# Decay attention, then two feed-forward stages, on one core: scores of the first eight head pairs by fp32 products, transposes on two row halves, reciprocals turned by VectorE

## The chip, the core and the metric

The kernel runs on one core of a Trainium2 chip. Its time is device microseconds (us) of one execution, and the number to move is the median over runs: 971.85 us before the change (three runs, 971.4 to 974.48). TensorE (PE) multiplies matrices into eight PSUM banks; VectorE (DVE), ScalarE (ACT) and GpSimd (POOL) work on tiles in SBUF and PSUM; SyncE (SP) issues the DMA transfers. Each engine runs its own list of instructions in order, and semaphores tie the lists together.

## The reference

Attention over 4 batches of 8 heads, 576 positions of 64 numbers each, with a decay that comes from gates f; then two feed-forward stages over 2304 rows.

```python
scores = np.matmul(q, k.transpose(0, 1, 3, 2)) / np.sqrt(D)      # D = 64, S = 576
cum = np.cumsum(np.log(np.clip(f, 0.0001, 1.0)), axis=-1)
scores = np.where(causal, -1e9, scores + cum[:, :, :, None] - cum[:, :, None, :])
attn = np.exp(scores - np.max(scores, axis=-1, keepdims=True))
x = np.matmul(attn / (np.sum(attn, axis=-1, keepdims=True) + 1e-09), v)   # -> 2304 x 512
...
x = act1(x @ w_in) @ w_out            # 512 -> 2048 -> 512
x = act2(x @ w_in2) @ w_out2          # 512 -> 2048 -> 512
```

## The kernel before

Two heads of one batch make a pair, and there are 16 pairs. The 576 queries of a head are five blocks: four of 128 and a last one of 64. The last blocks of both heads are stacked into one tile (`both` in the code), so a pair has nine tiles of 128 query rows. For each tile there are these steps, named as in the code:

- **S**, scores into PSUM (L460 for the stacked tile, L469 for the others). q and k were split beforehand into a high and a low fp32r part (`hi` on ACT, L415; `lo` on DVE or POOL, L419), and a score is three products, low x high, high x low and high x high. For the stacked tile q goes in with zeros beside each head (`diag`, L422), on all 128 rows of the array. For the other tiles the two heads have 64 contracted rows each, and two matmuls run on the two row halves of the array, into two banks. A tile takes only the keys up to its diagonal: 512, 384, 256 or 128.
- **M**, the row maximum (L509, DVE), which also adds the decay and the mask from the tile `cb`. Pair 0 has no `cb`: there the decay is a fourth product with the tile `ct`, which four small DMAs fill.
- **E**, the exponential with its row sum (L521, ACT).
- **T**, the transpose of the probabilities (L533, PE): per 128 keys one 128x128 fp32 matmul against the identity, into one bank; two such banks are in turn (`TB_` = 2). **C** copies the bank to SBUF, on ACT or DVE (L381, L383).
- **V**, probabilities by values (L570, PE), plain fp32, the two heads side by side on two column halves of the array; **O** copies the result out.
- **R**: reciprocals of the row sums (L594, L595), transposed on PE (L599), copied by ACT (L604), stored by one DMA (L607), loaded back broadcast over partitions (L614, L615) and multiplied in by POOL (L619).

Beside the attention PE has filler work: for the first two column chunks the first layer of stage one with four of its sixteen weight blocks (h, L758) and their share of the second layer (a, L839), 96 + 96 matmuls of 512 columns. Weights come as 64-bit numbers and are turned into fp32 by ACT and DVE (L93 to L113), much of it beside the attention. Then the two feed-forward stages follow (L758, L852, L854).

The order of the instructions on each engine is not the order of the code. Each step is a task with a key, a duration, what it depends on and which buffers it takes; a planner (`plan`) puts the tasks out by expected time and key, and `NUDGE`, a list of (first task, count, shift), moves keys. The emitted order is fixed; on the chip an engine waits where its next instruction is not ready.

At the start f is loaded, clipped (L655), turned into logarithms (L706) and summed up (L658); PE meanwhile runs 26 matmuls on zeros (L652).

Of the kernel before, what the change touches and what calls it, by code (L numbers as in the profile page):

```python
# [18 lines left out]
def kernel(ctx, tc, qT, kT, v, f, w_in1, w_out1, w_in2, w_out2, a, b, out):  # L19
# [21 lines left out]
    W_EARLY = 4  # L41
    W_MID = 5
# [4 lines left out]
    SB, TB_, OB, RB = 4, 2, 2, 2  # L47
    KM, KEX, KT, KC, KV, KR, KX, PKL, LK, FE, FS = 0.0, 1.0, 4.0, 4.0, 7.0, 2.0, 9.0, 7.0, 14.0, 170.0, 40.0
    I_K, I_Q = 4.4, 5.2
    CS = 12.0  # L50
    WARM, WARM2 = 12, 14
# [7 lines left out]
    ACT.preload_act_table_set("natural_log_exp_and_others")  # L59

    ident = const.tile([P, P], F32, name="ident")
    POOL.memset(ident[:], 1.0)
    POOL.affine_select(
        out=ident[:], in_=ident[:], compare_op=ALU.is_equal, fill=0.0, base=0,
        pattern=[[-1, P]], channel_multiplier=1,
    )
# [75 lines left out]
    def w_load(m, g, half):  # L142
# [19 lines left out]
    tri = ap1.tile([P, 512], F32, name="tri")  # L162
    tri2 = ap1.tile([P, 256], F32, name="tri2")
    POOL.memset(tri[:], 0.0)
    POOL.memset(tri2[:], 0.0)
    POOL.affine_select(
        out=tri[:, 384:512], in_=tri[:, 384:512], compare_op=ALU.is_ge, fill=-BIG, base=0,
        pattern=[[-1, P]], channel_multiplier=1,
    )
    for j in range(2):  # L170
        t = tri2[j * QB:(j + 1) * QB, 192:256]
        POOL.affine_select(
            out=t, in_=t, compare_op=ALU.is_ge, fill=-BIG, base=0, pattern=[[-1, QB]], channel_multiplier=1,
        )

    kt, qt = [[[ap1.tile([P, S], F32R, name=f"{x}{y}{n}") for y in "hl"] for n in range(2)] for x in "kq"]
    qd = [[ap1.tile([P, P], F32R, name=f"qd{y}{n}") for y in "hl"] for n in range(2)]


    cb = [ap1.tile([P, 3, S], F32, name=f"cb{n}") for n in range(2)]
    ct = [ap1.tile([P, S], F32R, name="ct0")]
# [3 lines left out]
    rt_ = [ap1.tile([P, P], F32, name=f"rt{n}") for n in range(2)]  # L190
    for n in range(2):
        POOL.memset(vt[n][0:QB, NC - 1, :], 0.0)
        POOL.memset(rt_[n][:], 0.0)
    one, oned = [ap1.tile([P, P], F32R, name=f"one{x}") for x in range(2)]
    half = ap1.tile([P, 2], F32, name="half")
    POOL.memset(half[:], 0.0)
    POOL.memset(oned[:].bitcast(F32), 0.0)
    for j in range(2):
        pp = slice(j * QB, (j + 1) * QB)
        POOL.memset(half[pp, j:j + 1], 1.0)  # L200
        POOL.memset(oned[j * QB:j * QB + 2, pp].bitcast(F32), 1.0)
    POOL.memset(one[:].bitcast(F32), 1.0)
    POOL.memset(ct[0][:].bitcast(F32), 0.0)
# [8 lines left out]
    def load_pair(pr, x):  # L212
        if x < 2:
            t = ap2.tile([P, S], F32, tag=("ks", "qs")[x], name=f"{'kq'[x]}s{pr}")
            SP.dma_start(t[:], (kT, qT)[x][pr])
        else:
            t = vt[pr % 2]
            SP.dma_start(
                t[:, 0:NC - 1, :], v[pr, 0:(NC - 1) * P, :].rearrange("(c p) d -> p c d", p=P)
            )  # L220
            SP.dma_start(t[QB:P, NC - 1, :], v[pr, (NC - 1) * P:S, :])
        nat[pr, x] = t

# [48 lines left out]
    MOVE, LAND = 1.4, 1.4  # L272
# [116 lines left out]
    xa = {}  # L389

    def tasks_of_pair(pr):
# [3 lines left out]
        c_ = ct[0]  # L395
# [25 lines left out]
        def diag(y, eng):  # L421
            ENGINES[eng].tensor_tensor(  # L422
                out=(qdh, qdl)[y][:].rearrange("p (x s) -> p x s", x=2),
                in0=(qh, ql_)[y][:, S - QB:S].bitcast(F32).unsqueeze(1).to_broadcast([P, 2, QB]),
# [6 lines left out]
        else:  # L431
            T("ldc", -99, "sp", [(0.55, 0.05)] * 4, lambda: load_c(pr), ((0, "c"),), ("cb",))
# [6 lines left out]
        T("qd0", kk + 3, ways, [0.24, 0.4], [lambda e=e: diag(0, e) for e in ways], ("qhi",))  # L439
        T("qd1", kk + 3, ways, [0.24, 0.4], [lambda e=e: diag(1, e) for e in ways], ("qlo",))  # L440
# [728 lines left out]
```

## Time and profile before

| | |
|---|---|
| median of three runs | 971.85 us (971.4 to 974.48) |
| span of the profiled execution | 969.2 us; the median is 2.65 us above it |
| PE busy | 956.1 us, 99% of the span |
| DVE, ACT, POOL busy | 707.6 us, 629.7 us, 436.0 us |
| last V ends, last filler follows | 215.15 us, to 220.94 us |
| from there to the end | PE busy 744.28 us of 745 us |

An engine's busy time counts an instruction from its start to its end, and matmuls overlap, so a busy PE may still be waiting between starts. How much a run of matmuls costs is read from start to start, or from the chain of work that ended last, in which each piece lasts until the next one starts.

### The profile page before, as it was taken

The page shows a single profiled execution, that of the slowest core. Times are in us where ns is not written, and L with a number is a line of the kernel's source. Part 1 is how long each engine was busy: PE and PEld are TensorE (multiplying, and loading weights), DVE is VectorE, ACT ScalarE, POOL GpSimd, SP SyncE. Part 2 cuts the span into 40 slices and gives each one's busy share as a digit, 9 for nine tenths or more (in the row PEclk, how much of TensorE's full clock was granted, in tenths as well). Part 3 has the DMA queues.
Part 4 walks back from the last instruction along what each step waited for, and adds up shares of the span by engine and source line. Part 5 has one row for each costly group of instructions (what it writes and reads, how often), then busy time and mean ns, then how long its engine had stood idle before and what let it go on. Part 6 is the DMA issues. An engine that isn't in the chain of part 4 may idle for free.

```text
span 969.2 us, 15465 instructions
## 1 busy us (share of the span) xinstructions
PE 956.1 (99%) x5124; PEld 783.1 (81%) x5124; DVE 707.6 (73%) x1391; ACT 629.7 (65%) x1327; POOL 436.0 (45%) x490
## 2 busy tenths in 40 slices
PE   8999999999999999999999999999999999999998
PEld 5667777778888888888888998888888888888887
DVE  7898889963878967867755779776666766766565
ACT  6999888875654434334334579777677677766675
POOL 3766745636455422322221235444445454444444
PEclk9999999999999999999999999999999999999999
DMA  7897798756553565755742650010101100010010
GB/s 231 256 287 236 230 284 283 246 174 197 189 192 110 163 209 161 238 174 158 244 131 88 196 168 7 1 44 0 44 12 33 44 1 23 0 44 1 1 44 23
DMA packets 66656, 125.14 MB, mean 129 GB/s; under 512 B 10048, under 2 KB 20944, under 8 KB 66576
## 3 DMA queue, kind: packets, MB, share of 16 engines
q1 hardware_dynamic: 66576, 124.16, 40.0%
q8 instruction: 40, 0.66, 0.3%
q14 instruction: 40, 0.33, 0.1%
HBM read 94.61 MB, written 29.51 MB: 128 GB/s over the span
## 4 chain that ended last, share of the span: by engine, by line
PE 80%; DVE 2%; ACT 1%; issue 0%; POOL 0%; ACTq 0%
PE h L758 38%; PE a L854 20%; PE a L852 17%; PE T L533 1%; PE O L570 1%; PE a L839 1%; PE S L469 1%; DVE wd L113 1%; DVE wd L107 0%; DVE wd L101 0%; PE S L460 0%; ACT wh L127 0%; ACT t L782 0%; DVE t L786 0%; POOL wl L131 0%
## 5 line engine op out<-in xcount | busy, mean ns | idle before, releaser
L772 POOL TENSOR_TENSOR gl<-t,gh 128x512 fp32r<-128x512 f32 (+1 forms) x160 | 196.3, 1228 | 278.7 <-ACT gh L768 202.2
L758 PE MATMUL h<-xh,wl 128*128 128x512 f32 (+1 forms) x640 | 236.9, 370 | 0.2 <-POOL wl L131 0.2
L758 PE MATMUL h<-xl,wh 128*128 128x512 f32 (+1 forms) x640 | 235.5, 368 | 0.0
L758 PE MATMUL h<-xh,wh 128*128 128x512 f32 (+1 forms) x640 | 235.5, 368 | 0.0
L768 ACT CAST gh<-t 128x512 fp32r<-128x512 f32 (+1 forms) x160 | 93.0, 582 | 117.1 <-PE a L854 47.2
L803 POOL TENSOR_TENSOR t<-t,t 128x512 f32<-128x512 f32 (+1 forms) x80 | 94.5, 1181 | 129.5 <-ACT t L796 121.2
L758 PEld LDWEIGHTS h<-xh,wl 128*128 128x128 f32 x640 | 120.6, 188 | 20.9 <-POOL wl L131 0.6
L758 PEld LDWEIGHTS h<-xh,wh 128*128 128x128 f32 x640 | 120.6, 188 | 20.0
L758 PEld LDWEIGHTS h<-xl,wh 128*128 128x128 f32 x640 | 120.7, 189 | 19.8
L854 PE MATMUL a<-wh,gl 128*128 128x512 f32 x288 | 112.2, 389 | 0.0
L854 PE MATMUL a<-wl,gh 128*128 128x512 f32 x288 | 112.2, 389 | 0.0
L854 PE MATMUL a<-wh,gh 128*128 128x512 f32 x288 | 112.0, 389 | 0.0
L852 PE MATMUL a<-gh,wl 128*128 128x512 f32 (+1 forms) x288 | 105.3, 366 | 0.0
L852 PE MATMUL a<-gl,wh 128*128 128x512 f32 (+1 forms) x288 | 105.3, 365 | 0.0
L852 PE MATMUL a<-gh,wh 128*128 128x512 f32 (+1 forms) x288 | 105.2, 365 | 0.0
L782 ACT ACTIVATE t<-t 128x512 f32<-128x512 f32 (+1 forms) x80 | 47.1, 589 | 75.8 <-DVE t L777 75.6
L777 DVE TENSOR_SCALAR t<-h 128x512 f32<-128x512 f32 (+1 forms) x80 | 50.8, 635 | 60.2 <-PE h L758 59.7
L821 DVE SCALAR_TENSOR_TENSOR t<-t,na,h 128x512 f32<-128x512 f32 (+1 forms) x80 | 55.3, 691 | 53.3 <-ACT h L817 52.4
L521 ACT ACTIVATE P<-P,nm 128x384 f32<-128x384 f32 (+3 forms) x144 | 84.1, 586 | 15.6 <-DVE nm L509 14.6
L807 DVE TENSOR_TENSOR t<-h,t 128x512 f32<-128x512 f32 (+1 forms) x80 | 51.0, 637 | 55.4 <-ACT t L799 55.1
L238 POOL TENSOR_SCALAR_AFFINE_SELECT cb<-cb 128x128 f32<-128x128 f32 (+1 forms) x150 | 56.2, 387 | 62.9 <-DVE nm L509 47.4
L793 ACT ACTIVATE t<-h,ab 128x512 f32<-128x512 f32 (+1 forms) x80 | 51.8, 649 | 43.5 <-PE h L758 43.5
(121 smaller groups left out, 1883.6 us busy)
## 6 DMA issues: line engine op xcount, KB each, us to landing
raw<-in_moe_w_in_dram SPq DMA_DIRECT2D x32, 512.0 KB, 3.7
raw<-in_moe_w_out_dram SPq DMA_DIRECT2D x32, 512.0 KB, 4.2
xr<-xd SPq DMA_DIRECT2D x48, 256.0 KB, 3.9
wfd<-wd SPq DMA_DIRECT2D x42, 256.0 KB, 4.2
wf<-wfd SPq DMA_DIRECT2D x42, 256.0 KB, 2.6
cb<-cd SPq DMA_DIRECT2D x15, 576.0 KB, 9.4
ks<-in_k_dram SPq DMA_DIRECT2D x16, 288.0 KB, 4.7
qs<-in_q_dram SPq DMA_DIRECT2D x16, 288.0 KB, 4.7
```

Source lines behind the costliest of these rows:

```text
L238: POOL.affine_select(out=t, in_=t, compare_op=ALU.is_ge, fill=-BIG, base=0, pattern=[[-1, n]], channel_multiplier=1,)
L521: ACT.activation(p, p, AF.Exp, scale=-1.0, bias=nm[pr][:, pos:pos + 1], accum_out=ls[pr][:, COL[pos]:COL[pos] + 1])
L758: PE.matmul(hps[g], ww[:, kk * P:(kk + 1) * P], xx[kk], start=(kk == 0 and y == 0), stop=(kk == KD - 1 and y == 2))
L768: ACT.copy(gt[g][0], mid[g][0])
L772: eng.tensor_tensor(out=lo, in0=mid.pop(g)[0], in1=hi.bitcast(F32), op=ALU.subtract)
L777: DVE.tensor_scalar(out=c, in0=hps[g], scalar1=-1.0, scalar2=1.0, op0=ALU.max, op1=ALU.min)
L793: ACT.activation(mid[g]["w"], hps[g], AF.Abs, scale=ab[:, 0:1])
L803: POOL.tensor_tensor(out=vv, in0=vv, in1=mid[g]["w"], op=ALU.add)
L807: DVE.tensor_tensor(out=t, in0=hps[g], in1=t, op=ALU.mult)
L821: DVE.scalar_tensor_tensor(out=t, in0=t, scalar=na[:, 0:1], in1=hps[g], op0=ALU.add, op1=ALU.mult)
L852: PE.matmul(acc[x, d], ww[:, dd], gg, start=st, stop=sp)
L854: PE.matmul(acc[x, d], gg[:, dd], ww[:], start=st, stop=sp)
```

## The change

For the first eight pairs (`WHOLE` = 8) q and k are not split. The scores are one fp32 product of the tiles as loaded; the stacked tile's q with zeros is one tile `qdw`, made from the loaded q. In pair 0 the decay is a second fp32 product of `sel` or `seld` (constants that pick a head's row and scale it) with the running sums, which stay in the tile where they are computed (`fr`), two copies of them on two partition halves. The four small DMAs and `ct` are gone. The first k and q are loaded by ACT's queue, f is loaded twice, and the fills of the constants move behind it on POOL.

The transposes of all pairs are issued in halves: 64 rows of the probabilities against a 64x64 identity, the two row halves into two banks. A T task now takes the two heads of a block together, into one tile of two banks (`TB_` = 1), and the next T task takes the same tile. The stacked tile's fifth chunk has no copy of its own any more.

The reciprocals are turned by VectorE in 32x32 blocks, and four DMAs store them; the transpose on PE and the copy on ACT are gone. The first warm-up has 9 matmuls for 12, and the second (14) is gone. The planner's durations and delays are set anew, and `NUDGE` has 60 other entries for 30.

```diff
+    WHOLE = 8
-    SB, TB_, OB, RB = 4, 2, 2, 2
+    SB, TB_, OB, RB = 4, 1, 2, 2
+    TD = 0.083
-    WARM, WARM2 = 12, 14
+    WARM, WARM2 = 9, 0
...
     NUDGE = [
-        (648, 29, -0.8), (1339, 23, 1.6), (1564, 5, 0.5), (1173, 66, -1.2), (4043, 36, 0.6), (240, 8, -16.0),
+        (1214, 20, 4.2), (1179, 11, 8.2), (1186, 22, 32.3), (1122, 21, 1.2), (655, 17, -2.9), (401, 1, 4.3),
...
+        if whole:
+            T("qd0", kk + 3, ways, [0.24, 0.4], [lambda e=e: diag(0, e) for e in ways], ("ldq",), ("qdw",))
-        for x, (nm_, tag) in enumerate((("k", "ks"), ("q", "qs"))):
+        for x, (nm_, tag) in enumerate((("k", "ks"), ("q", "qs")) if not whole else ()):
...
+                        if whole:
+                            ways = [(qdw[pr % 2][:], k_[:, n0:n1])] + ([] if pr else [(seld[:], cum[:, n0:n1])])
+                        else:
+                            ways = [(qdl[:], kh[:, n0:n1]), (qdh[:], kl_[:, n0:n1]), (qdh[:], kh[:, n0:n1])]
...
+                if whole:
+                    ways = [(q_[:, qc], k_)] + ([] if pr else [(sel[:], cum)])
+                else:
+                    ways = [(ql_[:, qc], kh), (qh[:, qc], kl_), (qh[:, qc], kh)]
...
-                    for c in range(c0, c1):
+            def t_fn(heads=heads, nch=nch):
+                tt = psT.tile([P, 2, 512], F32, tag="T", name=f"T{heads[0]}")
+                for jj, s_ in enumerate(heads):
+                    p = Pt.pop(s_)
+                    cc = slice(jj * nch * QB, (jj + 1) * nch * QB)
+                    Tt[s_] = tt[:, :, cc]
+                    for c in range(nch):
                         k0 = min(c * P, S - P)
-                        PE.transpose(ps[:, (c - c0) * P:(c - c0 + 1) * P], p[:, k0:k0 + P], ident[:])
+                        for h in range(2):
+                            r = slice(h * QB, (h + 1) * QB)
+                            PE.transpose(tt[:, h, cc.start + c * QB:cc.start + (c + 1) * QB], p[r, k0:k0 + P], ident[r, r])
...
-        def r2():
-            Rr[pr] = psT.tile([P, 512], F32, tag="T", name=f"rT{pr}")
-            PE.transpose(Rr[pr][:, 0:P], rt_[pr % 2][:], ident[:])
-        def r3():
-            ACT.copy(rr[:], ps[0:NB, 0:P])
+            Rr[pr] = ap2.tile([P, 32], F32, tag="rr", name=f"rr{pr}")
+            DVE.transpose(out=Rr[pr][:], in_=rt_[pr % 2][:])
         def r4():
-            SP.dma_start(rcd[pr].rearrange("(p s) -> p s", s=P), Rr.pop(pr)[:])
+            r = Rr.pop(pr)
+            for x in range(4):
+                SP.dma_start(rcd[pr].rearrange("(p a s) -> p a s", a=4, s=32)[:, x, :], r[x * 32:x * 32 + NB, :])
...
+    fr = cb[0]
+    SP.dma_start(fr[0:NH, 0, :], f_)
+    SP.dma_start(fr[QB:QB + NH, 0, :], f_)
...
+    def equal(t, base):
+        n = t.shape[1]
+        POOL.affine_select(
+            out=t, in_=t, compare_op=ALU.not_equal, fill=-ROOT, base=base, pattern=[[0, n]], channel_multiplier=1,
+        )
+    for t in (seld, sel):
+        POOL.memset(t[:], 0.0)
+        for j in range(2):
+            pp = slice(j * QB, (j + 1) * QB)
+            equal(t[pp, pp if t is seld else slice(0, P)], -j)
```

How the lists of the engines change is shown at three places. First, PE at its first scores. Before, the stacked tile of pair 0 (S) by q with zeros (qdl, qdh), k (kh, kl) and the decay (ct):

```order
L460 MATMUL S_0_224<-kh_115,qdl_124 128x320
L460 MATMUL S_0_224<-kl_116,qdh_123 128x320
L460 MATMUL S_0_224<-kh_115,qdh_123 128x320
L460 MATMUL S_0_224<-ct_129,one_139 128x320
L460 MATMUL S_320_229<-kh_115,qdl_124 128x256
```

The same tile now, with the loaded k (ks), qdw and the sums (in cb) by sel, and the next two tiles, which take the loaded q (qs):

```order
L436 MATMUL S_0_191<-ks_129,qdw_111 128x320
L436 MATMUL S_0_191<-cb_113,sel_123 128x320
L436 MATMUL S_320_194<-ks_129,qdw_111 128x256
L436 MATMUL S_320_194<-cb_113,sel_123 128x256
L449 MATMUL S_0_202<-ks_129,qs_131 128x512
L449 MATMUL S_0_203<-ks_129,qs_131 128x512
```

Four products of a tile have become two, and none of them needs ACT or the four DMAs. Second, PE beside a later pair, where the transposes of the pair in hand stand around the stacked scores of the next one. Before:

```order
L533 MATMUL T_0_2382<-ident,P_2264 128x128 x3
L533 MATMUL T_0_2390<-ident,P_2290 128x128 x3
L460 MATMUL S_0_2398<-kh_115,qdl_124 128x320
L460 MATMUL S_0_2398<-kl_116,qdh_123 128x320
L460 MATMUL S_0_2398<-kh_115,qdh_123 128x320
L460 MATMUL S_320_2402<-kh_115,qdl_124 128x256
L460 MATMUL S_320_2402<-kl_116,qdh_123 128x256
L460 MATMUL S_320_2402<-kh_115,qdh_123 128x256
L533 MATMUL T_0_2411<-ident,P_2362 128x128 x2
L533 MATMUL T_0_2419<-ident,P_2368 128x128 x2
```

Now, at the like place:

```order
L517 MATMUL T_2818<-ident,P_2699 128x64 x8
L517 MATMUL T_2818<-ident,P_2711 128x64 x8
L436 MATMUL S_0_2837<-kh_99,qdl_108 128x320
L436 MATMUL S_0_2837<-kl_100,qdh_107 128x320
L436 MATMUL S_0_2837<-kh_99,qdh_107 128x320
L436 MATMUL S_320_2841<-kh_99,qdl_108 128x256
L436 MATMUL S_320_2841<-kl_100,qdh_107 128x256
L436 MATMUL S_320_2841<-kh_99,qdh_107 128x256
L517 MATMUL T_2855<-ident,P_2759 128x64 x6
L517 MATMUL T_2855<-ident,P_2780 128x64 x6
```

A transpose of 128 columns has become two of 64, two heads write one tile, and the tile is taken again after one run of scores. Third, POOL at the start. Before, the fills of constants end with ct, and no score needs POOL before its mask:

```order
L201 MEMSET one_139 2x64 x2
L203 MEMSET ct_129 128x576
L238 AFFINE_SELECT cb_128<-cb_128 64x64 x2
```

Now the product of q and half that makes qdw stands behind all fills:

```order
L648 MEMSET tri 128x512
L649 MEMSET tri_120 128x256
L200 AFFINE_SELECT tri<-tri 128x128
L200 AFFINE_SELECT tri_120<-tri_120 64x64 x2
L653 MEMSET ident 128x128
L654 AFFINE_SELECT ident<-ident 128x128
L659 MEMSET vt_115 64x128
L660 MEMSET rt_117 128x32
...
L392 TENSOR_TENSOR qdw_111<-qs_131,half 128x128
```

The first score on PE waits for that product.

## Rows read from the trace of the kernel before

**Rows 1.** The page's head: span, and busy time of PE.

```profile
span 969.2 us, 15465 instructions
PE 956.1 (99%) x5124; PEld 783.1 (81%) x5124; DVE 707.6 (73%) x1391; ACT 629.7 (65%) x1327; POOL 436.0 (45%) x490
```

**Rows 2.** Windows: stretch, length, busy per engine (instructions), clock, DMA share, GB/s.

```profile
0.00:25.00 25.00, 22.37 (x134) 14.06 (x134) 18.70 (x54) 16.78 (x41) 8.25 (x31) 0.93 0.70 228
25.00:75.00 50.00, 46.18 (x377) 32.54 (x375) 45.47 (x147) 47.63 (x148) 35.40 (x62) 1.00 0.87 270
221.00:966.00 745.00, 744.28 (x3552) 627.19 (x3550) 522.67 (x829) 442.31 (x792) 312.13 (x256) 1.00 0.29 95
```

**Rows 3.** Chain that ended last, about pair 13: start, length until the next.

```profile
173.69 0.11 PE T L533
173.80 0.11 PE rT L599
173.91 1.42 PE S L469 x12
175.33 2.86 PE O L570 x28
...
178.89 0.84 PE S L469 x12
...
182.34 0.81 PE S L460 x6
...
215.15 5.79 PE a L839 x24
```

**Rows 4.** Groups of PE by form: the transposes.

```profile
L533 PE MATMUL T<-ident,P 128*128 128x128 f32 x400 | 63.9, 281 | 5.0 <-ACT PT L381 3.2 <-DVE PT L383 1.1 <-ACT rr L604 0.2
```

**Rows 5.** Timeline of PE and its weight loads at 101 us: start, length.

```profile
101.58 0.28 PE L469 MATMUL S<-kl,qh 64*128 64x128 f32 x2
101.69 0.28 PE L469 MATMUL S<-kh,qh 64*128 64x128 f32 x2
101.91 1.09 PE L533 MATMUL T<-ident,P 128*128 128x128 f32 x8
102.76 0.48 PE L758 MATMUL h<-xh,wl 128*128 128x512 f32 x1
...
101.91 0.86 PEld L533 LDWEIGHTS T<-ident,P 128*128 128x128 f32 x8
```

**Rows 6.** Timeline of the first 12 us.

```profile
3.90 1.35 DVE L658 TENSOR_TENSOR_SCAN ft<-ft,zt 32x576 f32<-32x576 f32 x1 [0.75 <-ACT ft L706]
4.68 0.58 POOL L203 MEMSET ct<- 128x576 f32 x1
7.00 2.48 SPq L233 DMA_DIRECT2D ct<-ft  x4
9.10 0.39 PE L460 MATMUL S<-kh,qdl 128*128 128x320 f32 x1 [0.28 <-ACT qh L415]
10.78 0.39 PE L460 MATMUL S<-ct,one 66*128 66x320 f32 x1 [1.00 <-DMA ct<-ft]
```

**Rows 7.** Groups of ACT, DVE and POOL by form, first 215 us.

```profile
L381 ACT COPY PT<-T 128x512 f32<-128x512 f32 x34 | 19.2, 579 | 1.1 <-PE T L533 1.0
L415 ACT CAST qh<-qs 128x576 fp32r<-128x576 f32 x16 | 10.7, 671 | 0.0
L604 ACT COPY rr<-rT 9x128 f32<-9x128 f32 x16 | 4.0, 247 | 0.1
L383 DVE COPY PT<-T 128x512 f32<-128x512 f32 x14 | 9.5, 686 | 1.2 <-PE T L533 1.0
L422 POOL TENSOR_TENSOR qdh<-qh,half 128x128 fp32r<-128x128 f32 x12 | 5.5, 458 | 5.8 <-ACT qh L415 5.7
```

**Rows 8.** Windows at the start, columns as in rows 2.

```profile
5.00:11.80 6.80, 5.52 (x28) 2.91 (x28) 4.68 (x11) 3.73 (x6) 0.27 (x1) 0.99 0.44 141
11.80:15.20 3.40, 3.40 (x19) 2.57 (x18) 2.49 (x9) 1.75 (x5) 0.00 (x0) 0.51 0.95 255
```

More of the change, by code (lines that the diff above doesn't have):

```diff
@@ L159 @@
     psH = psA = psO
+    kt, qt = [[[ap1.tile([P, S], F32R, name=f"{x}{y}{n}") for y in "hl"] for n in range(2)] for x in "kq"]
+    qd = [[ap1.tile([P, P], F32R, name=f"qd{y}{n}") for y in "hl"] for n in range(2)]
+    qdw = [ap1.tile([P, P], F32, name=f"qdw{n}") for n in range(2)]
+    cb = [ap1.tile([P, 3, S], F32, name=f"cb{n}") for n in range(2)]
+    vt = [ap1.tile([P, NC, P], F32, name=f"vt{n}") for n in range(2)]
+    rt_ = [ap1.tile([P, 32], F32, name=f"rt{n}") for n in range(2)]
     tri = ap1.tile([P, 512], F32, name="tri")
     tri2 = ap1.tile([P, 256], F32, name="tri2")
[L164 to L186, printed above, removed]
-    vt = [ap1.tile([P, NC, P], F32, name=f"vt{n}") for n in range(2)]
[L190 to L194, printed above, removed]
-    half = ap1.tile([P, 2], F32, name="half")
[L196 to L203, printed above, removed]
+    half = ap1.tile([P, 2], F32, name="half")
+    sel, seld = [ap1.tile([P, P], F32, name=f"sel{x}") for x in range(2)]
     BLOCKS = [(LAST, None)] + [(b, j) for b in reversed(range(LAST)) for j in range(2)]
@@ L394, in tasks_of_pair @@
         (kh, kl_), (qh, ql_), (qdh, qdl), cb_ = (t[pr % 2] for t in (kt, qt, qd, cb))
-        c_ = ct[0]
+        whole = pr < WHOLE
         def T(name, key, eng, dur, fn, deps=(), take=(), free=()):
@@ L478, in tasks_of_pair @@
             else:
[L479 to L482 removed]
+                np_ = 3 if not whole else 4 if pr else 8
+                dur = np_ * sum(mm(n1 - n0) for n0, n1 in cuts) + 0.05 if both else np_ * max(mm(w), 0.11 if whole else 0.095) - 0.01
+                deps = ("ldk", "ldq", "qd0", prev) + (() if pr else ("c",)) if whole else ("klo", "qlo", "qd0", "qd1", prev)
+                free = (("qdw",) if whole and both else ()) + ((("ks", "qs") if whole else ("k", "q")) if pos == NB - 2 else ())
+                T(f"S{pos}", s, "pe", 0.02 + dur, s_fn, deps, ("S", "S"), free)
                 if not both:
@@ new lines, in tasks_of_pair, with c_fn @@
+            if both or j == 1:
+                t = f"T{pos}"
+                T(t, s + KT, "pe", TD * nch * len(heads), t_fn, [f"E{pos - x}" for x in range(len(heads))] + [(pr, lastT[0]) if pos else (pr - 1, lastT[0])], ("T", "T"), ("P",) * len(heads))
+                lastT[0] = t
+                shape[tid[pr, t]] = "rows"
+            def c_fn(eng, s=s, g=g, j=j, qo=qo, nch=nch, both=both):
+                if (pr, g) not in PT:
+                    PT[pr, g] = ap1.tile([P, 2 + 3 * g, 2, GQ[g]], F32, tag=f"PT{g}", name=f"PT{pr}_{g}")
+                to, src = PT[pr, g], Tt.pop(s).rearrange("p h (c x) -> p c h x", x=QB)
+                if both:
+                    copy(eng, to[:, 0:nch, :, qo:qo + QB], src)
+                else:
+                    copy(eng, to[:, 0:nch, j, qo:qo + P].rearrange("p c (h x) -> p c h x", x=QB), src)
@@ new lines, in tasks_of_pair @@
+            engs = ["act", "dve"]
+            for pos_, j_, s_ in [(pos, j, s)] if both else [(pos - 1, 0, s - 1), (pos, 1, s)] if j else []:
+                T(f"C{pos_}_0", s_ + KC, engs, [cost(e, nch * P, "ps") for e in engs],
+                  [lambda e=e, f=c_fn, j_=j_, s_=s_: f(e, s=s_, j=j_) for e in engs], (t, f"PT{g}"),
+                  (f"PT{g}",) if firstg and pos_ == pos - len(heads) + 1 else (), ("T", "T") if both else ("T",))
+                if firstg and pos_ == pos - len(heads) + 1:
+                    tid[pr, f"PT{g}"] = tid[pr, f"C{pos_}_0"]
@@ L644 @@
     DVE.memset(zt[:], 0.0)
-    load_pair(0, 0)
-    load_pair(0, 1)
+    DVE.memset(fr[NH:QB, 0, :], 1.0)
+    POOL.memset(fr[QB + NH:P, 0, :], 1.0)
+    POOL.memset(half[:], 0.0)
+    for j in range(2):
+        POOL.memset(half[j * QB:(j + 1) * QB, j:j + 1], 1.0)
+    def equal(t, base):
[5 more added lines that the diff above has]
+        POOL.memset(t[:], 0.0)
+        for j in range(2):
+            pp = slice(j * QB, (j + 1) * QB)
+            equal(t[pp, pp if t is seld else slice(0, P)], -j)
+    POOL.memset(tri[:], 0.0)
+    POOL.memset(tri2[:], 0.0)
+    no_later(tri[:, 384:512])
+    for j in range(2):
+        no_later(tri2[j * QB:(j + 1) * QB, 192:256])
+    POOL.memset(ident[:], 1.0)
+    POOL.affine_select(
+        out=ident[:], in_=ident[:], compare_op=ALU.is_equal, fill=0.0, base=0,
+        pattern=[[-1, P]], channel_multiplier=1,
+    )
+    for n in range(2):
+        POOL.memset(vt[n][0:QB, NC - 1, :], 0.0)
+        POOL.memset(rt_[n][:], 0.0)
     def warm(n):
-        ps = psT.tile([P, 512], F32, tag="T", name="warm")
+        ps = psT.tile([P, 2, 512], F32, tag="T", name="warm")[:, 0, :]
         for _ in range(n):
```

133 lines of the change are left out of this document (45 added, 88 removed), and 15 rows, old and new, of the table NUDGE.

## The prediction

> **What bounds the kernel now.** I read the page's head first: PE is busy 956.1 us of a span of 969.2 [rows 1]. The windows say where that is real [rows 2]. From 221 us to the end PE is busy 744.28 of 745 us, and the change touches nothing there, so all it can do lies in the first 221 us. From 25 to 75 us three engines are nearly full at once: PE 46.18, ACT 47.63 and DVE 45.47 of 50. Then the chain of work that ended last: at pair 13 it goes from one PE piece to the next, with no wait between them [rows 3]. So what leaves PE's list there comes off the end one for one, while in the first 75 us an edit must relieve PE, ACT and DVE together.
>
> I work against the profiled execution, span 969.2 us. The median of the runs, 971.85, is 2.65 us above it, and I take that distance as kept. A measurement of this kernel can tell about 0.3%, 3 us, from no change.
>
> **Transposes.** There are 400 of 128 columns [rows 4]. Eight take from 101.91 to 102.76, and a single one in the chain takes 0.11 us, so I price one at 0.11 [rows 3, 5]: 44 us in all. Each becomes two of 64 columns on two row halves. Nothing before runs such a pair, so I bound it. Below: V runs fp32 on two halves of the array at once. Its 28 instructions are 14 matmuls, each issued twice, over 2 x (3 x 320 + 192 + 64) + 2 x (256 + 128) = 3200 columns, so 6400 columns of instructions in 2.86 us [rows 3]. Two halves of 64 columns would be 128 of these, 0.057 us. Above: the narrowest scores, two row halves with 128 columns of weights each, follow at 0.11 us (101.58 to 101.69) [rows 5], which saves nothing. The new pair streams as few columns as V's narrowest and loads as many weight columns as these scores, so I take the middle, 0.08: 400 x 0.03 = 12 us saved, with ends at 21 and 0.
>
> A rule speaks against this. Eight weight loads take 0.86 us, and so do eight transposes up to the next matmul (0.85), so loads are hidden beside the matmul before them on the same rows [rows 5]. The Trainium skill (TensorE: Matmul & The Clock Gate, sections LDWEIGHTS and What overlaps and what doesn't) has a load take its columns / 1.2 ns, 107 ns for 128 however few the rows, and overlap a running matmul only where the row groups differ. By it a half's load could not hide behind the same half's matmul: an estimate of 0.107 + 0.053 = 0.16 us a pair, which makes the sum 32 us worse. The trace disagrees, since by that rule the 128-column transposes would need over 0.2 us. A weaker form of it stays among the rivals.
>
> **Scores.** A pair's three products take 0.81 us for the stacked tile and 1.42 + 0.84 for the others, 3.07 us [rows 3]. As one fp32 product, by V's rate (2.86 / 6400 = 0.00045 us per column and instruction on two halves, double that on the whole array): the stacked tile 2 x 576 x 0.00089 = 1.03; the 512 and 384 tiles 4 x 896 x 0.00045 = 1.60; the 256 and 128 tiles 4 x 384 x 0.00045 = 0.69. That is 3.32. The 3.07 contains changes of the array's form, and one costs about 0.11: from the last scores to T at 101.91 there is 0.22 where 0.11 is the pace [rows 5]. With two of these, 3.5 us, so 0.45 more in each of pairs 1 to 7: +3.2 us. Pair 0 had four products, 4.1 us by the same rows, and gets two fp32 ones, 6.8: +2.7. Together +5.9, ends 4.3 (no changes of form) and 8.
>
> Changes of form in the lists, up to the last filler, are 110 before and 101 now: the transposes no longer share a form with the fillers and the stacked scores, but share one with the other scores. I cost that at nothing; nine at 0.11 are 1 us.
>
> **Reciprocals.** The 16 transposes on PE at 0.11 go: -1.8 us [rows 3]. VectorE's block transpose is not in the trace; I put it between nothing and the 0.247 us of the copy that goes [rows 7], so at most 4 us on DVE, covered by DVE's idle time (5 of 50 us in the fullest stretch [rows 2]). The 48 more DMA issues, at 2.48 / 4 = 0.62 us [rows 6], are 30 us of SP's queue over 215 us. They are hidden as long as loads are issued some microseconds ahead; uncovered, a pair's next k and q come 1.9 us late.
>
> **Start.** The first score starts at 9.10 us, and the decay's product then waits 1.0 us for ct [rows 6]. Now the sums are ready where the scan leaves them, at 5.25 us [rows 6], or some 0.4 later with a second load of f in front. The later input is qdw: POOL's fills end at 5.26 [rows 6], their number is about the same now, and qdw stands behind them at 0.46 [rows 7], so about 5.9 to 6.6. First score at 6.4: -2.7, and the 1.0 goes: -3.7 us. Queued behind qdw on POOL are the masks of pair 1, which have time. The granted clock stood at 0.51 from 11.8 to 15.2 us, the lower level, after a stretch in which PE was busy 5.52 of 6.8 us [rows 8]. The warm-up is shorter and the first scores earlier; I expect such a stretch again and count no change. Half of 3.4 us, 1.7, is what it may give or take.
>
> **Relief of ACT and DVE.** ACT loses 16 splits at 0.671 (10.7 us) and 16 copies at 0.247 (4.0 us) [rows 7]; DVE and POOL lose 16 subtractions and 8 products. All of the splits lie in the first eight pairs, where ACT is full. PE is idle 3.8 us from 25 to 75 us [rows 2], and its matmuls hide more waiting between starts; I take 3 us back, ends 0 and 6.
>
> **The shared T tile.** This adds a wait. The next T task needs both copies of the last one: 0.58 us on ACT beside 0.69 on DVE [rows 7], behind the last transpose's 0.28 [rows 4], 0.97 in all. In the pattern of the lists the stacked scores alone stand between, 0.81 us [rows 3]: short by 0.16. Of 79 successions I count a quarter so: +3 us, where the waits for these copies so far come to 3.2 + 1.1 [rows 4]. Ends are 0 and 20. Queued behind a waiting T on PE are all scores, and behind those the maxima on DVE.
>
> **Sum.** -12 + 5.9 - 1.8 - 3.7 - 3 + 3 = -11.6: span 957.6, so 960 us.
>
> **Rivals.**
>
> *The halves run as V does.* 0.057 a pair gives 9 us more, and with scores at their lower end and 1 us more relief the time is 949. For it: the two halves of V and of the scores do run together, and a transpose's load is short (eight in 0.86 us). Against it: nothing shows two 128-column loads in 0.057 us.
>
> *The halves don't pay.* The pace stays at 0.11 per pair, as for the narrowest scores; the 12 us are gone: 972, no change.
>
> *The shared tile decides.* Where a copy starts late, because ACT or DVE is in another instruction of 0.6 us when T ends, PE stands still: there are no second banks to go on with. If three in four of the 79 successions lose 0.35 us, that is 21 us in place of 3: 978, slower. It decides from about 0.2 us lost per succession on average, where it eats the whole gain. For it: ACT is busy 47.63 of 50 us [rows 2]. Against it: ACT is relieved there, and after 75 us fillers and V often stand between. The Trainium skill (TensorEngine Tiling (Array Packing), section PSUM Bottleneck) warns of the same: after tiling, the copy out of PSUM may bound; no row here shows how far.
>
> *The loads don't hide.* A half's load of 0.86 / 8 = 0.107 us [rows 5], followed by its matmul's 0.057, is 0.16 a pair; the transposes take 64 us, 32 more than I forecast: 992. Against it: loads hide so far [rows 5].
>
> **How the numbers follow.** My forecast, 953 to 967, has 0.57; the halves as V 0.20; no pay 0.11; the shared tile 0.09; the loads 0.03. The first two are faster by over 0.3% (below 969): 0.77. No pay is the same, 0.11. The last two are slower, 0.12. The range leaves out what is below the best of the bounds, the slower cases and a little of the no-pay case: 945 to 972.
>
> **What would show it.** T's records in pairs of 64 columns, about 0.08 us from pair to pair; S of pairs 1 to 7 at about 3.4 us a pair; a first score near 6.4 us; fewer PE waits from 25 to 75 us; the last V near 203 us in place of 215; the stretch after the last filler as long as before. I am wrong if T pairs stand 0.11 apart, if waits of T for the copies in PT come to over 10 us, or if the stages behind the attention change their length.

## The result: slower, 981.2 us

The changed kernel takes 981.22 us (980.02 to 981.96, four runs) against 971.85, a ratio of 1.0094 with a 95% interval of 1.0078 to 1.0111. The forecast was 960. In the profiled execution the span is 978.3 us where it was 969.2 [rows 1]. The page's head after, and the windows that answer to [rows 2]; the matmul behind the last filler now starts at 228.9 us instead of 220.8, so the third window begins later:

```profile
span 978.3 us, 16019 instructions
PE 945.5 (97%) x5421; PEld 764.9 (78%) x5421; DVE 711.9 (73%) x1391; ACT 617.3 (63%) x1272; POOL 428.1 (44%) x490
```

```profile
0.00:25.00 25.00, 20.17 (x120) 10.89 (x121) 12.53 (x42) 12.11 (x31) 8.38 (x33) 1.00 0.72 215
25.00:75.00 50.00, 42.27 (x452) 25.95 (x448) 42.81 (x144) 42.22 (x128) 27.51 (x56) 1.00 0.76 232
229.00:975.00 746.00, 744.77 (x3553) 627.11 (x3551) 530.50 (x832) 444.24 (x793) 312.63 (x258) 1.00 0.30 96
```

PE is busy 10.6 us less than before, and yet the end is 9.1 us later. From 25 to 75 us all of PE, ACT and DVE have become less busy (PE 42.27 of 50, before 46.18): PE is idle twice as long there, 7.7 us instead of 3.8, where fewer waits were forecast. From 229 us on PE is as full as before, as foreseen.

The transposes' group by form [rows 4], and a place where ten of them (five pairs) stand between two scores, in PE's timeline at 15 us (start, length):

```profile
L517 PE MATMUL T<-ident,P 64*128 64x64 f32 x800 | 43.0, 234 | 22.6 <-ACT PT L348 12.9 <-DVE PT L350 8.0 <-DVE rt L702 1.1
```

```profile
15.66 0.47 PE L517 MATMUL T<-ident,P 64*128 64x64 f32 x10
15.97 0.45 PE L449 MATMUL S<-ks,qs 64*128 64x256 f32 x2
```

Five pairs from 15.66 to 15.97 are 0.062 us a pair, where a whole transpose took 0.11 [rows 5]. But the waits of T for the copies into PT are 12.9 + 8.0 us, where they were 3.2 + 1.1. The waits of PE give their count (total, times, longest), together 20.9 us, twice the 10 us that the prediction had named as a sign of being wrong:

```profile
PE T L517 <- ACT PT L348: 12.9, 18, 2.1
PE T L517 <- DVE PT L350: 8.0, 11, 2.1
```

One of these waits, in the timeline of PE, ACT and DVE at 141 us. The T tile holds two heads, and ACT copies both:

```profile
139.22 0.46 PE L517 MATMUL T<-ident,P 64*128 64x64 f32 x8 [0.61 <-DVE PT L350]
139.61 2.27 PE L557 MATMUL O<-PT,vt 128*64 128x320 f32 x20
...
141.23 0.69 ACT L88 ACTIVATE wd<-raw 128x512 f32<-128x512 f32 x1 [2.26 <-DMA raw<-in_moe_w_out_dram]
141.83 0.34 ACT L348 COPY PT<-T 128x256 f32<-128x256 f32 x1
142.08 0.77 ACT L499 ACTIVATE P<-P,nm 128x576 f32<-128x576 f32 x1
...
142.85 0.35 ACT L348 COPY PT<-T 128x256 f32<-128x256 f32 x1
...
143.25 0.34 PE L517 MATMUL T<-ident,P 64*128 64x64 f32 x4 [1.36 <-ACT PT L348]
```

T has ended at 139.68. PE goes on with V (the O line), has run dry at 141.89 and stands until the second copy has ended, 1.36 us later. Both copies together are 0.69 us. What makes them late is what stands ahead of them in ACT's list: a weight conversion that has waited 2.26 us for its DMA and holds up the first copy until 141.83, and then an exp between the two, so that the second begins 1.02 us behind the first.

I add up PE's time by kind of work for the kernels that matter, from each matmul's start to the next one's, with the idle gap between its end and the next start taken apart. "Ends" is where the matmul behind the attention stage's last filler starts:

| kernel | T and rT | scores | V | fillers | warm-up | idle | ends |
|---|---|---|---|---|---|---|---|
| before | 52.8 | 55.7 | 48.1 | 47.4 | 7.6 | 7.9 | 220.8 |
| changed | 33.0 | 68.3 | 48.8 | 46.4 | 4.0 | 27.0 | 228.9 |
| t_full_shared | 53.0 | 66.4 | 48.0 | 45.4 | 4.0 | 16.4 | 234.5 |
| t_full_two | 54.0 | 65.3 | 47.8 | 45.6 | 4.0 | 9.9 | 227.9 |
| two_one | 52.9 | 65.6 | 47.9 | 45.3 | 4.0 | 5.5 | 222.5 |
| b_turn | 52.2 | 56.3 | 48.1 | 47.9 | 7.9 | 11.4 | 225.2 |
| b_whole | 53.5 | 59.3 | 47.5 | 47.5 | 7.8 | 8.2 | 224.9 |

The changed kernel's T work is 19.8 us less; scores take 12.6 more; idle time 19.1 more.

At the start, PE's timeline (answering to [rows 6]), and then DVE and POOL just before it in the changed kernel and in t_full_two, a run of the section below whose lists begin with the same steps:

```profile
7.71 1.44 PE L436 MATMUL S<-ks,qdw 128*128 128x320 f32 x2 [2.43 <-POOL qdw L392]
8.94 1.27 PE L436 MATMUL S<-cb,sel 128*128 128x320 f32 x2
10.00 1.06 PE L436 MATMUL S<-ks,qdw 128*128 128x256 f32 x2
10.86 1.06 PE L436 MATMUL S<-cb,sel 128*128 128x256 f32 x2
11.85 1.83 PE L449 MATMUL S<-ks,qs 64*128 64x512 f32 x4
```

```profile
6.11 1.36 DVE L672 TENSOR_TENSOR_SCAN cb<-cb,zt 128x576 f32<-128x576 f32 x1 [0.75 <-ACT cb L713]
...
6.37 0.12 POOL L660 MEMSET rt<- 128x32 f32 x1
6.46 1.20 POOL L392 TENSOR_TENSOR qdw<-qs,half 128x128 f32<-128x128 f32 x1
```

```profile
6.39 1.75 DVE L673 TENSOR_TENSOR_SCAN cb<-cb,zt 128x576 f32<-128x576 f32 x1 [0.75 <-ACT cb L714]
...
6.53 0.39 POOL L392 TENSOR_TENSOR qdw<-qs,half 128x128 f32<-128x128 f32 x1
```

The first score starts at 7.71 us, not at 6.4. POOL's fills last until 6.46, not 5.26, and qdw, right behind them, takes 1.20 us, where pair 1's takes 0.40. VectorE's scan runs beside it. In t_full_two qdw takes 0.39 and the scan 1.75 instead of 1.36: each time one of the two is longer, as if they did not run at once. The sums are ready at 7.47, not at some 5.65.

### The profile page after: what moved, and what is told of

Its sections match the earlier page's. It is cut to its first block, busy times and chain, and to the rows that moved or that the text cites. A ratio compares the mean times of both kernels' runs of the same rounds, so it can differ in the third digit from the quotient of the medians.

```text
span 978.3 us, 16019 instructions
## 1 busy us (share of the span) xinstructions
PE 945.5 (97%) x5421; PEld 764.9 (78%) x5421; DVE 711.9 (73%) x1391; ACT 617.3 (63%) x1272; POOL 428.1 (44%) x490
## 4 chain that ended last, share of the span: by engine, by line
PE 77%; DMA 11%; DVE 4%; issue 2%; ACT 2%; SPq 2%; POOL 2%; POOLq 0%; DVEq 0%; ACTq 0%
PE h L763 37%; PE a L859 20%; PE a L857 17%; DMA cb<-cd 3%; DMA R<-rcd 2%; DMA rcd<-rr 1%; DVE P L487 1%; ACT P L499 1%; DMA vt<-in_v_dram 1%; DMA wfd<-wd 1%; DVE PT L350 1%; PE S L436 1%; DMA xd<-xa 1%; DMA raw<-in_moe_w_in_dram 1%; SPq L596 1%
## 5 line engine op out<-in xcount | busy, mean ns | idle before, releaser
L499 ACT ACTIVATE P<-P,nm 128x384 f32<-128x384 f32 (+2 forms) x144 | 83.8, 584 | 17.2 <-DVE nm L487 15.1
L812 DVE TENSOR_TENSOR t<-h,t 128x512 f32<-128x512 f32 (+1 forms) x80 | 51.0, 637 | 53.5 <-ACT t L804 52.1
L487 DVE CUSTOM_DVE_ANT_0 P<-S,cb 128x256 f32<-128x256 f32 (+1 forms) x135 | 62.4, 477 | 12.0 <-POOL cb L200 10.4
```

Source lines behind the costliest of these rows:

```text
L487: DVE.tensor_tensor_reduce(out=p[:, n0:n1], in0=t[:, 0:n1 - n0], in1=m, scale=-1.0 / ROOT, scalar=least, op0=ALU.add, op1=ALU.min, accum_o ...
L499: ACT.activation(p, p, AF.Exp, scale=-1.0, bias=nm[pr][:, pos:pos + 1], accum_out=ls[pr][:, COL[pos]:COL[pos] + 1])
L812: DVE.tensor_tensor(out=t, in0=hps[g], in1=t, op=ALU.mult)
```

## The experiments

Theories at the outset: S, the shared tile; Q, the reciprocals' new way and SP's queue; L, the list. Ratios are to the kernel before on the same chip, with 95% intervals; differences in us are of medians. Names with b_ keep the order of before; the others keep the changed order, except after_nolist and after_warm, where another list or another length of the warm-up gives another plan. b_noturn, one_noturn and two_noturn leave a step out, so their output is not that of the reference.

**The tile and the halves.** In both, `PE.transpose` takes 128 columns again; in the first into the shared two-bank tile, in the second into tiles of one bank:

```
t_full_shared  PE.transpose(tt[...128 columns...], p[:, k0:k0+P], ident[:])
t_full_two     for c0 in range(0, nch, 4): t1 = psT.tile([P, 512], F32, tag="T")
```

> The changed kernel with its order and its shared two-bank T tile, but whole transposes of 128 columns in place of the halves. T's own time on PE rises by some 400 x 0.05 = 20 us. If PE's work bounds the stage: about 1000. If the waits bound it (theories S and Q): the longer transposes lie partly in the time that T waits, but the copies also start later; Q says 983 to 990, S says 990 to 1000 because each copy, and so each next T, moves back by the longer T.

> The same whole transposes in the same order, but each head's T in a one-bank tile of its own, two in turn as before the change (the stacked tile's fifth chunk in a second bank, with a copy of its own). Compared with the run with the shared tile it undoes the sharing alone. Theory S: T's waits for copies fall from over 20 us to under 10, time 10 us or more below the shared run. Theory Q: within 4 us of the shared run.

t_full_shared 985.32 us, 1.0158 [1.0131, 1.0185]; t_full_two 978.77 us, 1.0090 [1.0061, 1.0119]. PE's waits in the two, t_full_shared first:

```profile
PE T L515 <- ACT PT L348: 9.0, 13, 2.5
PE T L515 <- DVE PT L350: 4.5, 9, 0.8
```

```profile
PE T L516 <- DVE PT L350: 3.1, 3, 2.2
...
PE T L516 <- ACT PT L348: 1.2, 2, 0.8
```

Sharing one tile costs 6.5 us at the same work (without it there is even one copy more per pair). On the shared tile, the halves take 20 us of T off PE (53.0 to 33.0) and bring the end 4.1 us nearer (985.32 to 981.22): 10.6 us of them turn into idle time. T's waits fall to 4.3 us without the sharing, as theory S has it, but the price is smaller than S had it (10 us or more, and t_full_shared above 990): 985.3 lies where Q had it. And without any sharing the kernel is still slower than before, so there is more.

**One store instead of four.**

```
-rcd = dram.tile([NPAIR, 2 * S])   +rcd = dram.tile([NPAIR, 32 * P])
-for x in range(4): SP.dma_start(rcd[pr]...[:, x, :], r[x * 32:x * 32 + NB, :])
+SP.dma_start(rcd[pr].rearrange("(p a s) -> a p s", a=4, s=32), r[:])
```

> The changed kernel with its order kept, but the turned reciprocals of a pair go out in one DMA (all 128 rows of the tile, 32 numbers each, into a wider scratch row) and not in four: 48 fewer DMA issues on SP. Theory Q (the reciprocals' way is late: four stores and the loads behind them hold up SP, POOL's multiply waits for R, and the masks, maxima, exponentials and copies behind it come late): POOL's wait for R falls from 24.8 us to under 12, PE's wait of T for copies from 20.9 to about 10, time about 970. Theory S (the shared T tile alone: the copies need that long whatever SP does): T's waits stay at 19 to 22 us, time 979 to 983.

one_store 978.43 us, 1.0072 [1.0045, 1.0098], 2.8 us less. T still waits 11.2 + 7.4 us, and POOL still waits 31.8 us for R (37.8 in the changed kernel, by the same view), so theory Q alone falls. The stores are a smaller part of it.

**The list.** `NUDGE = []`.

> The changed kernel with an empty list of key shifts. Theory L (the 60 shifts fit the planner's model and not the chip, and the slower time is theirs): 970 or below. Theories S and Q: the order is less fitted, 981 to 1000.

988.10 us, 1.0177 [1.0156, 1.0199]. The list is worth 7 us, so theory L as it was put falls. What another list would give is not shown.

**The parts one by one in the order of before.** b_turn adds `DVE.transpose(out=Rr[pr][:], in_=rt_[pr % 2][:])` behind the reciprocals and the four stores, and drops TensorE's turn and ScalarE's copy; b_turn_one has the one store; b_whole has the fp32 products in pairs 1 to 7 (`ways = [(qdw, ks)]`, and `kk_, qq = ks, qs`), without the splits.

> The kernel before with one part of the change: VectorE turns the reciprocals in 32x32 blocks and four DMAs store them; TensorE's turn and ScalarE's copy are gone; order, T tiles and scores stay. Theory Q (four stores on one queue cost some 3 us wherever they stand): +1 to +4 us over the kernel before, and xa at L601's counterpart waits over 15 us for R in all (before 4.6). Theory L (they cost only where SP's queue is already late, as in the changed kernel): -2 us, as the prediction's term had it (-1.8), with R waits under 8 us.

> As b_turn with one store of the turned block instead of four. Theory Q: 2 to 4 us less than b_turn, so -2 us against the kernel before. Theory L: within 1 us of b_turn.

> The kernel before with another part alone: pairs 1 to 7 take their scores by one fp32 product of q and k as loaded; the rounded copies and remainders of these pairs are not made; order, T tiles and reciprocals stay, the k and q buffers are three instead of two. Theory P (TensorE is full, so its work is the price; the changed kernel's TensorE spent some 0.95 us more per such pair): +4 to +8 us. Theory A (ScalarE and VectorE are late and get some 3 us per pair back): -3 to 0 us.

> The changed kernel with whole 128-column transposes into two one-bank tiles in turn, and one store of the turned reciprocals: what is left of the change is the fp32 scores, the turned reciprocals and the list. If the shared tile and the four stores add: 778.8's counterpart t_full_two (978.8 us) less the 2.8 us that one store gave = 976 us; what is left over 972 is then the scores' share. If the stores only mattered because the shared tile made T late: 978 to 979 us, as t_full_two.

b_turn 978.82 us, 1.0077 [1.0060, 1.0093]; b_turn_one 976.87, 1.0050 [1.0027, 1.0073]; b_whole 974.58, 1.0038 [1.0020, 1.0056]; two_one 974.12, 1.0024 [1.0014, 1.0033]. The surprise is b_turn: the part that I had put at -1.8 us costs 7.7 by itself, more than either theory had, and 5.7 with one store, where Q had a gain. b_whole follows theory P: summed pair by pair, its pairs 1 to 7 take PE 28.4 us of scores where before takes 23.7, 4.7 more, and the end comes 3.4 later by the medians. The table shows 3.6 because pair 0, whose products are the same in both, takes 4.9 in b_whole and 6.0 in the profile of before, where the granted clock stood at 0.51 from 11.8 to 15.2 us [rows 8]. ACT and DVE, relieved of the splits (from 25 to 75 us ACT is busy 41.4 us and DVE 36.7, before 47.63 and 45.47), bring the end no nearer. two_one is 2 us under its first expectation; PE idles 5.5 us only and carries 9.9 us more of scores.

**VectorE or the stores?** b_noturn is b_turn_one with `Rr[pr] = rt_[pr % 2]` in the place of VectorE's turning; b_store4 is the kernel before with its rr stored by four DMAs of 32 columns.

> b_turn_one without VectorE's turning: the reciprocals are stored as they stand by one DMA of the same size (so rows get other queries' reciprocals; the work of the rest is the same). Theory D (VectorE's added 0.21 us per pair, in the chain between the last exp of a pair and the next pair's maxima, is the price): within 1 us of the kernel before, so 3 to 5 us under b_turn_one. Theory Q (the store and the queue): within 1 us of b_turn_one, 976 to 977 us.

> The kernel before, reciprocals turned by TensorE and copied by ScalarE as there, but stored in four DMAs instead of one. Theory Q: +2.5 us (the step from b_turn_one to b_turn was 1.9). Theory D: within 1 us of the kernel before, since VectorE has no more to do.

b_noturn 970.96 us, 0.9990 [0.9981, 0.9999]; b_store4 975.18, 1.0034 [1.0025, 1.0043]. Both theories hold, each for its share: VectorE's turning some 6 us (b_turn_one less b_noturn; the runs of b_turn_one spread from 973.9 to 980.4, so by the intervals 3 to 8), the three further stores 2 to 3.6. And b_noturn, in which TensorE's turn and ScalarE's copy are gone and nothing has come in their place, is only 0.6 us faster than the kernel before. SP's timeline in the kernel before and in b_store4 shows what the stores take of its queue:

```profile
44.78 0.29 SPq L607 DMA_DIRECT2D rcd<-rr  x1
45.19 0.35 SPq L215 DMA_DIRECT2D ks<-in_k_dram  x1
```

```profile
44.59 1.52 SPq L609 DMA_DIRECT2D rcd<-rr  x4
```

The next pair's k stands behind them, 1.2 us later. Elsewhere in the stage the four take 1.35 to 3.4 us.

**Place or amount?** The turning is busy for 16 x 0.211 = 3.4 us. b_turn_late and one_late are b_turn_one and one_store with the same turning issued later:

```
 def r1(): ... DVE.reciprocal(r, r)
-    DVE.transpose(out=Rr[pr][:], in_=rt_[pr % 2][:])
 def r3():    # r4 in one_late
+    DVE.transpose(out=Rr[pr][:], in_=rt_[pr % 2][:])
```

> b_turn_one with VectorE's turning issued where ScalarE's copy stood, so one to three of the next pair's maxima go ahead of it; same work, same single store. If the place is the price: 971 to 973.5 us. If the amount is: within 1.5 us of b_turn_one, 975.5 to 978.5 us.

> one_store with the turning issued just ahead of its store in the written order. If the place is the price: 973 to 975.5 us, as one_noturn. If the amount is: 977 to 980 us, as one_store.

b_turn_late 973.09 us, 1.0013 [1.0004, 1.0021]; one_late 975.68, 1.0036 [1.0025, 1.0046]. The place is most of the price: the later place gives back 3.8 of the 6 us, and 2.8 in the changed order, where one_late lies just above the range of the place. DVE's timeline around the end of pair 3, in the kernel before, in b_turn_one and in b_turn_late:

```profile
54.16 0.21 DVE L595 RECIPROCAL rt<-rt 128x9 f32<-128x9 f32 x1
54.29 0.36 DVE L383 COPY PT<-T 128x256 f32<-128x256 f32 x1
54.64 0.69 DVE L509 CUSTOM_DVE_ANT_0 P<-S,cb 128x512 f32<-128x512 f32 x1
```

```profile
54.77 0.22 DVE L595 RECIPROCAL rt<-rt 128x9 f32<-128x9 f32 x1
55.02 0.21 DVE L597 STREAM_TRANSPOSE rr<-rt 128x32 f32<-128x32 f32 x1
55.16 0.38 DVE L383 COPY PT<-T 128x256 f32<-128x256 f32 x1
55.46 0.68 DVE L509 CUSTOM_DVE_ANT_0 P<-S,cb 128x512 f32<-128x512 f32 x1
```

```profile
53.84 0.22 DVE L595 RECIPROCAL rt<-rt 128x9 f32<-128x9 f32 x1
53.97 0.36 DVE L383 COPY PT<-T 128x256 f32<-128x256 f32 x1
54.25 0.68 DVE L509 CUSTOM_DVE_ANT_0 P<-S,cb 128x512 f32<-128x512 f32 x1
...
56.91 0.20 DVE L602 STREAM_TRANSPOSE rr<-rt 128x32 f32<-128x32 f32 x1
57.04 0.51 DVE L509 CUSTOM_DVE_ANT_0 P<-S,cb 128x384 f32<-128x384 f32 x1
```

Behind the reciprocal, the copy into PT follows at 0.13 us. The turning, which reads what the reciprocal writes, follows at 0.25, and the copy at 0.39: 0.26 us later, for a copy that T waits for and ahead of the next pair's first maximum. The 0.25 stands at all 16 ends of pairs in b_turn_one. Right behind the turning stands a copy into PT at five of them, a maximum at three, and work for weights or a later pair at eight. 16 x 0.26 is 4.2 us; how the delay reaches PE at the ends without such a copy is not shown. Placed later, the turning follows an unrelated instruction and costs 0.13 (56.91 to 57.04). I had taken the cover to be DVE's idle time; that idle time lies elsewhere in the stretch.

**The same turning in the changed order.** one_noturn and two_noturn leave it out of one_store and two_one; two_pe is two_one with TensorE's turn and ScalarE's copy, put ahead of the next transposes.

```
 def t_fn(heads=heads, nch=nch):
+    PE.transpose(ps[:, 0:P], rt_[x % 2][:], ident[:]); ACT.copy(r[:], ps[0:NB, 0:P])   # two_pe
```

> one_store (the changed kernel with one store) without VectorE's turning; the reciprocals are stored unturned, so rows get other queries' reciprocals. Theory D (VectorE's 0.21 us per pair stands in the chain of every order): 3 to 5 us under one_store, 973.5 to 975.5 us. Theory O (it costs only in the order of before, which was planned without it): within 1.5 us of one_store, 977 to 980 us.

> two_one (whole transposes in two tiles in turn, one store) without VectorE's turning, the reciprocals stored unturned. Theory D: 969 to 971 us. Theory O: 973 to 975 us.

> two_one with the reciprocals turned by TensorE and copied by ScalarE again (one store): of the change the fp32 scores, the start and the list are left. If the turning by VectorE costs here what it costs in the order of before (b_turn_one: +4.9 us): 969 to 970 us, under the kernel before. If the changed order, which was planned with it, hides it: 973.5 to 975.5 us, as two_one or 1 us more for TensorE's work.

one_noturn 973.92 us, 1.0028 [1.0017, 1.0039], 4.5 us under one_store by the medians, as theory D has it; the profiled spans of the two (973.5 and 973.7) do not show it, since that execution of one_store was its fastest. two_noturn 974.67, 1.0028 [1.0012, 1.0044]: no gain over two_one, so there D fails. two_pe 982.58, 1.0105 [1.0080, 1.0131], a miss: ACT now waits for TensorE in its list,

```profile
ACT rr L514 <- PE rT L512: 8.1, 12, 1.8
```

and what stands behind it waits too. This run says what that place costs, not what another would.

**The start.** `WARM, WARM2 = 12, 14` instead of `9, 0`.

> The changed kernel with as many warming products before the first scores as the kernel before (12 and 14 instead of 9 and none). Theory W (the first pair's fp32 products ran at the lower clock, 9.75 us where 6 would do, and that lost the earlier start): granted clock near 1 from the first score, pair 1 starts 1 to 3 us sooner than 19.9, the whole -1 to -3 us. Rival: the products delay the first score as much as the clock gives back: within 1 us.

990.93 us, 1.0195 [1.0165, 1.0225]. Both theories missed: 9.7 us slower, and pair 1 starts at 22.06, 2.1 us later. The planner counts the warm-up, so everything behind 12 us stands in another order, and the total says little about the start; the first microseconds do. The same five rows as above:

```profile
9.79 0.70 PE L436 MATMUL S<-ks,qdw 128*128 128x320 f32 x2
10.33 0.70 PE L436 MATMUL S<-cb,sel 128*128 128x320 f32 x2
10.87 0.59 PE L436 MATMUL S<-ks,qdw 128*128 128x256 f32 x2
11.30 0.59 PE L436 MATMUL S<-cb,sel 128*128 128x256 f32 x2
11.83 1.13 PE L449 MATMUL S<-ks,qs 64*128 64x512 f32 x4
```

Begun 2.08 us later, the eight instructions of the stacked tile end 0.02 us earlier. They take 2.04 us, and 4.14 in the changed kernel: twice the pace, as the clock's levels of 2.4 and 1.2 GHz would have it. In the changed kernel the warm-up had ended at 5.28 and PE had been idle for 2.43 us; in after_warm it had warming products to do up to the first score. So in this execution the earlier first score was worth nothing.

The idle stretch does not settle it alone. In after_nolist PE's list begins with the same products behind the same nine warming ones, and the stacked tile ran at the full pace behind an idle stretch as long:

```profile
7.69 0.81 PE L424 MATMUL S<-ks,qdw 128*128 128x320 f32 x2 [2.42 <-POOL qdw L380]
...
9.83 1.13 PE L437 MATMUL S<-ks,qs 64*128 64x512 f32 x4
```

Of the eleven profiled executions with nine warming products, nine ran the stacked tile at the lower pace in whole or in part (3.09 to 4.14 us), and after_nolist and t_full_two did not; in these two pair 1 starts at 17.21 and 17.14, in the changed kernel at 19.94. All nine profiled executions with 26 warming products ran their stacked tile, of other products but in after_warm, at the full pace. What decides between the two levels behind the short warm-up is not shown.

**A turn that no engine does.** One DMA writes each of the 1152 words to its turned place: `SP.dma_start(rcd[pr, 0:NB * P].rearrange("(p s) -> s p", s=P), rt_[pr % 2][:, 0:NB])`.

> The kernel before; the reciprocals go unturned to DRAM by one DMA that writes each word to its turned place (1152 words of 4 bytes), so neither TensorE, ScalarE nor VectorE turns anything. If the DMA lands within some 3 us of its issue and takes SP under 1 us: as b_noturn, 970.5 to 971.5 us. If words of 4 bytes are slow (over 6 us to land or over 2 us of SP's time): 974 us or more, xa waiting for R as in the changed kernel.

> two_one with the scattering store in the place of VectorE's turning. If theory D holds and the DMA is quick: 969 to 971 us, the only version here that would be under the kernel before with the fp32 scores. If D fails: as two_one, 974 us. If the DMA is slow: over 976 us.

b_scatter 1062.93 us, 1.0956 [1.0917, 1.0994]; two_scatter 1082.60, 1.1137 [1.1120, 1.1155]. SP is done with the issue in 0.38 us, but the loads of R, and what stands behind them in SP's list, then wait for the words (SP's timeline, and SP's waits over the stage):

```profile
43.82 0.38 SPq L604 DMA_DIRECT2D rcd<-rt  x1
...
54.42 0.45 SPq L611 DMA_DIRECT2D R<-rcd  x1
```

```profile
SPq L611 <- DMA rcd<-rt: 62.6, 9, 10.3
```

The Trainium skill (VectorE: DVE Perf Modes, section The three transpose paths) warns that a plain DMA copy which transposes by its strides is many times slower than the crossbar's transpose when the stride of the destination is large. The 10.6 us from the store's issue to the load's are of the slow way alone; no run here has the crossbar's, so the ratio is not shown. The mean granted clock of the two runs is 0.96, where the other runs here have 0.99 to 1.00: part of their time is PE at the lower level.

No kernel here with all of the computation beats the kernel before; b_turn_late comes nearest. The halves with two tiles in turn were not tried: S, T and O take all eight banks. Nor were the halves alone measured in the order of before.

## Why the prediction was wrong

The steps that failed are the shared tile's +3 and the reciprocals' -1.8, then the scores' +5.9, and behind these the relief's -3 and the start's -3.7. By the table, the end of the attention was forecast at -11.6 us and came at +8.1: T and rT gave 19.8 us instead of 13.8, the scores took 12.6 more instead of 5.9, and all the rest together, idle time above all, came to +15.3 instead of -3.7.

- **Transposes, -12.** Better than forecast on PE: 0.062 us a pair, near the lower bound 0.057, and 17.2 us less of T (50.2 without rT, to 33.0). The rule of the Trainium skill (TensorE: Matmul & The Clock Gate, sections LDWEIGHTS and What overlaps and what doesn't) by which a pair would need 0.16, by the estimate of the prediction, does not hold in these rows. On the path only some 4 us of it were left (t_full_shared to the changed kernel).
- **The shared tile, +3.** The step "the stacked scores alone stand between, short by 0.16, a quarter so" failed in its price, less in its count: 29 waits of 79 instead of 20, but 0.72 us each (20.9 / 29). I counted both copies as if they began when T ends; in the rows at 141 us the first begins 2.15 us behind T's end and the second 1.02 us behind the first, with other work of ACT ahead of each. That is the mechanism of the rival "the shared tile decides", which had 21 us lost and a time of 978, where 981.2 was measured; of the 20.9 us of waits 4.3 were there before. Yet that a rival comes near does not prove it the one cause: t_full_two, without the sharing, is nearly as slow. The tile is 6.5 us of it.
- **Reciprocals, -1.8.** Measured alone +7.7 (b_turn). Two steps failed: "covered by DVE's idle time" (0.26 us late, 16 times) and the issues "hidden as long as loads are issued some microseconds ahead" (b_store4, +3.6). I had their price and the condition, and took the average of a window for the cover. The gain itself was less too: 0.6 us in b_noturn, though the 16 turns had taken 2.6 us of PE's time (52.8 less 50.2).
- **Scores, +5.9.** Too small by half: +12.6. Pairs 1 to 7, put at +3.2, take 4.7 more in the order of before (b_whole) and 6.5 more in the changed one (30.2 us, before 23.7); I had priced them by pair 13's 3.07 us, and they took 3.4 each. Pairs 8 to 15, whose products did not change, take 28.3 us, before 26.0. What comes with the changed order, 1.8 and 2.3 us, I had put at nothing under changes of form. There PE's scores of pairs 1 to 15 stand in 62 separate runs instead of 48, and a run's first product is slower: 0.27 us against 0.17 for the next (starts at 143.40, 143.67 and 143.84 us). How much of it that is, is not shown. Pair 0 takes 9.7 us instead of 6.0, put at +2.7: its first scores ran at the clock's lower level, which I had counted as no change.
- **Relief of ACT and DVE, -3.** Nothing came (b_whole). From 25 to 75 us both have less to do there, and the end comes later by what PE has more; why the relief gives nothing is not shown further.
- **Start, -3.7.** 1.4 us of it came at the first score: the sums and qdw, put at 5.65 and 5.9 to 6.6 us, are ready at 7.47 and 7.66. Nothing of it is left at the end of the stacked tile (11.85 us, before 11.57), since that ran at the lower pace; pair 1 starts at 19.9 us, before at 18.8.
- **Behind the stage.** 749.4 us after the last filler, before 748.4: as forecast, within 1 us.

The parts don't add: b_turn (+7.7), b_whole (+3.4), the sharing (+6.5) and the halves (-4.1) make 13.5, measured 9.4; how much of the difference is the list that was made for the changed kernel is not shown. Open is why leaving the turning out of two_one gives nothing, when it gives 4.5 in one_store and 6 in the order of before.

## What to carry to other kernels

Work that is taken off the fullest engine is worth only what its next input allows: before counting on it, take the buffers that the edit removes and look in the lists for what stands ahead of the copies that release a tile, not at the durations of these copies. A small instruction that is added to an engine must be priced at its place (what it reads, and what stands right behind it), since idle time elsewhere in the window does not cover it; moving it down the list (past six instructions at the end of pair 3) was worth 3.8 of 6 us here. And an earlier start can be lost at once if the engine has meanwhile gone to its lower clock, as in the execution shown here.

## What was not expected of the hardware

- Two transposes of 64 columns on two row halves, into two banks, follow in 0.062 us together, each with a 128-column weight load.
- VectorE's 32x32 turning takes 0.21 us for 128x32 words, but starts 0.25 us behind the start of a reciprocal whose output it reads, where an unrelated copy starts after 0.13.
- Four small stores take 1.52 us of SP's queue in the rows shown, one takes 0.29; a store of 1152 single words holds up the load that reads them for 10 us.
- GpSimd's 128x128 product takes 1.20 us beside VectorE's scan and 0.39 or 0.40 otherwise; where it started 0.14 us behind the scan and took 0.39, the scan took 1.75 us instead of 1.36.
- The window from 7.70 to 10.80 us of the changed kernel is given with a granted clock of 1.00, while its products follow at half the pace of after_warm's:

```profile
7.70:10.80 3.10, 3.09 (x6) 2.19 (x7) 0.00 (x0) 0.48 (x1) 0.00 (x0) 1.00 0.45 105
```

The pace of equal products tells the level in this window, and the column does not.
